# One core's attention and gated convolution with its hand-written order of operations exchanged for another, and part of its casts, copies and sums on other engines

## The chip, the cores and the metric

The kernel runs on one core of a Trainium2 chip. A core has four compute engines that work at the same time, each in the order of its own instruction list: TensorE (PE in the profile, with its weight loads shown as PEld), VectorE (DVE), ScalarE (ACT) and GpSimd (POOL). SyncE (SP) issues most of the DMA transfers. The engines wait for each other by semaphores. What is measured is the device time of one execution in microseconds (us); less is better.

## The reference

Attention over four batches of eight heads, 768 positions and 64 channels a head, and behind it a gated convolution. Heads marked in `is_retrieval` (0, 2 and 6) attend causally to all earlier keys; the others only to the first four keys and a window of the last 64.

```python
def _attn_ref(q, k, v, is_retrieval, n_sink, window):
    scores = scale * np.matmul(q, k.transpose(0, 1, 3, 2))
    ...
    scores = np.where(mask[None, :, :, :], scores, -1000000000.0)
    scores = scores - np.max(scores, axis=-1, keepdims=True)
    a = np.exp(scores)
    a = a / (np.sum(a, axis=-1, keepdims=True) + 1e-09)
    return np.matmul(a, v).astype(np.float32)

def _moe_ref(x, w_proj, filter_fft, w_out):
    proj = x @ w_proj
    x1, x2, x3 = (proj[..., :D].copy(), proj[..., D:2 * D].copy(), proj[..., 2 * D:].copy())
    X2 = np.fft.rfft(x2, n=S, axis=1)
    H = np.fft.rfft(filter_fft, n=S, axis=0)[None, :, :]
    x2_conv = np.fft.irfft(X2 * H, n=S, axis=1)
    y = x1 * x2_conv * x3
    return (y @ w_out).astype(np.float32)
```

All inputs and the output are float32; the flags are integers.

## The kernel before

**The fast path and its fallback.** `patterned` computes everything for the one pattern of retrieval heads that it was written for. At its end a flag `other` says whether the inputs had that pattern and whether the sums of the softmax were sane; all engines load it (L1314) and jump over the general path `general` if it is zero, as here, and meet at the closing barrier (L1394).

**The order is written out by hand.** Each operation of `patterned` is a small function with a name. The string `FAST` (L63 to L124) lists 994 names, and the loop over its words (L1307) calls them in that order, so the order of the words is the order of the instructions on every engine. A word may carry an engine letter behind a slash (`s`, or none, ACT; `v` DVE; `p` POOL) and a PSUM slot behind an @ sign (four slots of two banks each, shared by all tiles that TensorE writes). Operations that are tied to one engine have no letter. For the helper `scaled` (L687) a `p` is the same as no letter. No engine looks ahead in its list: an instruction that waits holds up all behind it on that engine. DMA issues stand in the list as well, on SP (loads and stores), POOL (weights and filter) or, for some last stores, ACT.

**Attention.** Heads are worked in 16 pairs `n` (four per batch; pair `n` belongs to batch `n // 4`), both heads of a pair beside each other on 64 rows. For a pair: loads `lq`, `lk`, `lv` on SP; casts `cq`, `ck` of q and k to bf16 (both in one, `cqk`, from pair 8 on), cast `cv` of v; copies `vx`, `vs` and `ks` set up the values and keys of the window and of the first four positions; `T` turns q and k so that channels lie on partitions. Pairs 0 to 7 are turned by TensorE (`T0.0`, `T0.1`, with the evictions `E0.0`, `E0.1` from PSUM), pairs 8 to 15 by a transposing DMA that SP issues (L962, one word `T12`). `sc12.1` are the score matmuls of one chunk (L990, 64 rows), `sb` adds the mask by matmul for the first four pairs, `ex` is the exponential on ACT (L1007), `mk` and `mr` the mask by product on DVE for the others (L1017 to L1037), `at` the product with the values (L1050), `rec` the reciprocal of the sums (L1056) and `nm` the division on DVE (L1067), which gives the tile f_attn.

**The transform.** The Fourier transform over the 768 positions is done by matmuls on sums and differences: `fd` and `fe` fold f_attn into halves, `fA`, `fS`, `fb` and `fr` fold these again for pairs 5 to 15, `W` (L1103 to L1111) multiplies with the tables and `We` evicts. In parallel `tn` turns f_attn back (by TensorE up to pair 10, by DMA after) and `te` evicts it into f_xT. Per batch `b`: `X` (L1154) projects in the transformed domain, `Xe` evicts, `pa`, `pb` and `pc` multiply with the filter's transform (tile f_HAB), `c` (L1227) transforms back, `ce` and `cv` (with two more indices) join the halves. `x1` and `x3` (L1189) are the other two projections, `xs` evicts x1, `g` and `y` form the gated product f_gy, `o` (L1262) multiplies by w_out, `oe` evicts and `st` stores.

**The filter.** `lfilt` (L776) loads 768 KB on POOL's queue. `fold0` and `fold1` (L793, L797, DVE) fold it, `F` (L805) transforms it, `H0.0` to `H2.2` (L691 on DVE, L693 on ACT) evict it scaled into f_HAB. `lw` loads w_proj in six parts, also from POOL.

**The end.** `rest` (L586) runs eight matmuls on zeros behind the last real ones. `gd0` to `gd4` (L655 to L674) work out the flag: three steps on DVE, a small matmul `gd3`, a last step `gd4`.

Of the kernel before, what the change touches and what calls it, by code (L numbers as in the profile page):

```python
# [78 lines left out]
sw0.1 lv6 E7.1/s sc6.0@1 nm5/v sc7.0@2 pa0.0/p H2.3 pa0.2/v rec4 ex6.0 x10.0.0@3 x10.0.1 ex7.0 x30.0.0@1 nm4/v H2.4
x30.0.1 xs0.0/s lq8 cv6/p sc7.1@2 lv7 ex7.1 ks7/s sc6.1@0 x10.2.1@3 pa0.1/v ex6.1 g0.0 ks6/p pb0.2/v x10.2.0 tn4@1  # L80
xs0.2/s vs6/s x30.2.0@2 lk8 fe5/p te4/v sc6.4@0 sc6.2@3 pc0.2/v pb0.0/v x10.1.1@1 fd5/v ex6.2 mk6.2 x10.1.0 Gk1 fS5/v
ex6.4 fA5/v x30.2.1 x10.3.1@3 sc7.2@0 xs0.1/s g0.2 sc6.3@1 cqk8/s x10.3.0 pc0.1/v ex6.3 fd4/v fr5 x30.1.1@2 fb5/v
xs0.3/s x30.1.0 c0.1.0@1 lk9 lq9 T8 ex7.2 mk6.0 fe4/p pc0.0/v W4.1@3 ce0.1/s mk6.1 mr6 cv7/s W4.0 g0.1 vx6/v We4/s
# [5 lines left out]
x11.0.1@2 fr6 x11.0.0 T9 oe0.3/s at8.0@1 at8.1 lq11 fS7/v fA7/v oe0.1/s fr7 xs1.0/s chk cv9/v vx9/v sc9.1@0 fb6/p
fb7/v rec8 T10 lv10 nm8/v fe8/p sc9.0@3 x11.3.1@2 x11.3.0 W7.1@1 ex9.1 W7.0 W6.0@0 fd8/p ks9/p ex9.0 xs1.3/v W6.1  # L90
sc10.4@3 sc10.3@2 cqk11/p We6/v mk9.1 vs9/s We7/s sc10.0@1 lv11 ex10.4 ex10.3 sc9.2@3 mk9.0 ex9.2 X1.1.1@0 mk9.2 T11
tn8@2 X1.1.0 fS8/v ex10.0 Xe1.1/s X1.2.0@3 at9.1@1 te8/s at9.0 sc10.1@0 ks10/p X1.2.1 fA8/v ex10.1 Xe1.2/s sc11.0@2
rec9 sc11.1@0 cv10/v cv11/p nm9/v st0.1 x31.0.1@1 mk10.1 lk12 ex11.0 fd9/p ex11.1 x31.0.0 X1.0.1@3 lq12 sw1.1 lv13
# [5 lines left out]
fS10/p fA10/p lk13 ex12.4 x12.0.1 ex12.0 x32.0.0@3 pb1.0/v lv12 fb10/p pc1.0/v xs2.0/s sc12.5@1 sc12.2@0 fd11/v  # L99
sc12.3@2 x32.0.1 ex12.5 c1.0.0@1 c1.0.1 ex12.2 fr10 fA11/v lq15 fS11/v W10.1@0 W10.0 ex12.3 fr11 c1.1.0@2 c1.1.1  # L100
fb11/p g2.0 ce1.0/s c1.2.0@3 We10/s ce1.1/s W11.0@0 cv1.0.1 cv13/p cv1.0.0 mk12.1 cv1.1.0 cv1.1.1 c1.3.1@1 cqk13/s
W11.1 c1.3.0 y1.1/v y1.0/v ce1.3/v lk14 We11/s c1.2.1 ce1.2/s cv1.3.0 X2.1.0@2 lk15 T13 cv1.3.1 cqk14/s cv1.2.1
cv12/s X2.0.0@0 X2.1.1 mk12.0 X2.0.1 x31.3.0@1 T14 mk12.2 Xe2.1/s x31.3.1 Xe2.0/s cv1.2.0 y1.3/v sc13.1@3 vs13/s
ex13.1 sc13.0@2 g1.3 cqk15/p at12.1@0 at12.0 pa2.0/p sc14.1@1 rec12 sc14.0@3 ex13.0 nm12/v vx13/s X2.2.0@2 y1.2/v
ks13/s X2.2.1 pb2.0/v o1.1.0@0 ex14.1 pa2.1/v T15 lv15 mk13.1 o1.1.1 ex14.0 sc13.2@1 sc15.0@3 mk13.0 pc2.0/v ks14/p
Xe2.2/s fe12/v ex13.2 sc15.1@2 mk13.2 o1.0.0 st0.5 ex15.0 o1.0.1 x12.3.0@1 pa2.2/v x12.3.1 pb2.1/v at13.1@3 ex15.1
at13.0 ks15/p tn12 oe1.1/s fd12/v rec13 xs2.3/s lv14 exp0 o1.4.0@2 o1.5.0 fS12/v sc14.4@0 nm13/v sw2.1 fA12/v
sc15.2@1 fe13/v sc14.3@3 fd13/v st0.3 ex14.4 sc14.2@0 ex15.2 o1.4.1 ex14.3 o1.5.1 x12.2.1@1 mk14.1 fS13/v fr12 ex14.2
fA13/v x12.2.0 cv14/v sw2.0 vs14/s cv15/v x12.1.0@3 o1.2.0@0 tn13 xs2.2/s mk15.0 vx15/s st1.1 mk14.0 o1.3.0 fb13/v
vs15/v fb12/v x12.1.1 oe1.5/s W12.1@1 mr14 mk15.1 fr13 mk14.2 W12.0 o1.3.1 o1.2.1 vx14/s at14.0@2 xs2.1/s mk15.2  # L110
W13.1@3 W13.0 st1.5 We12/s at14.1 oe1.3/s at15.0@1 pc2.1/v pb2.2/v We13/s at15.1 rec14 rec15 pc2.2/p x32.1.0@0
x32.1.1 nm14/v c2.1.0@3 nm15/v c2.1.1 tn14 st1.3 ce2.1/s g2.1 cv2.1.1 cv2.1.0 c2.0.0@2 ce2.0/s c2.2.1@1 fd14/p y2.1/v
c2.3.1@0 fe15/p c2.3.0 c2.2.0 ce2.3/s fd15/v x32.2.1@3 cv2.3.1 cv2.3.0 fe14/p c2.0.1 x32.2.0 cv2.0.1 tn15 fS15/p
fS14/p fA14/p x32.3.1@0 cv2.0.0 x13.1.1@2 fA15/p ce2.2/s x13.1.0 g2.2 x32.3.0 xs3.1/s fr14 fb15/v y2.0/v fb14/v
W14.0@3 W14.1 x13.0.1@2 We14/s cv2.2.0 fr15 x13.0.0 W15.0@3 W15.1 cv2.2.1 x33.0.1@1 We15/v x33.0.0 y2.2/p X3.2.1@3
X3.2.0 xs3.0/s Xe3.2/s X3.1.1@2 y2.3/v g3.0 X3.1.0 X3.0.1@1 sw3.1 g2.3 Xe3.1/s sw3.0 X3.0.0 x13.2.1@0 pa3.1/v Xe3.0/s
o2.1.0@3 x13.3.0@2 o2.0.0 pa3.2/p x33.2.0@1 x13.2.0 pb3.1/p x13.3.1 pb3.2/v gd0 pc3.2/v o2.1.1 xs3.2/s pa3.0/v
pb3.0/v x33.2.1 x33.1.0@0 pc3.1/v o2.0.1 xs3.3/s g3.2 c3.0.0@2 pc3.0/p x33.1.1 c3.1.0@1 oe2.1/s ce3.0/s o2.4.0@3 g3.1
# [1280 lines left out]
```

## Time and profile before

| | us |
| --- | --- |
| Median of 3 runs | 185.31 |
| Lowest and highest of them | 184.15 and 185.63 |
| Span of the profiled execution, first to last instruction | 182.1 |

The profile is of one execution; it gives the span of its instructions, and which of the runs it was, or what lay around the span in it, it doesn't say. The median lies 3.2 us above the span.

Busy time is given for each engine as a share of that span. Rows that name a line (L1189) give engine, operation, the tile written and the tiles read, the shape, how many there were, busy time in all and the mean of one in nanoseconds, and behind the second bar how long the engine had been idle before them and what ended it. `f_` stands before the names of the tiles. The chain of waits goes back from the last instruction to whatever released each step. In this profile the order of the list leaves no gaps on TensorE of more than a few tenths but these: the opening up to 14 us, some around 17 to 25 us, and one ahead of sc12.1 at 103 us.

### The profile page before, as it was taken

The numbers are of one execution on the slowest core, as the hardware profiler recorded it, in microseconds if no ns is written. First come the engines' busy times: TensorE is split into PE (matmuls) and PEld (weight loads), VectorE is DVE, ScalarE is ACT, GpSimd is POOL, SyncE is SP. The second block draws the span as 40 slices with busy tenths as digits, with TensorE's granted clock in tenths as the row PEclk, the third lists the DMA queues.
The fourth block names the chain that finished last, engine by engine and source line by source line (L and its number), as shares of the span: only waits on it lengthen the run. The fifth ranks groups of instructions, "written<-read, shape, count | busy, mean of one in ns | idle before, by whom it ended". The sixth has DMA issues, their size and how long they took to land.

```text
span 182.1 us, 4374 instructions
## 1 busy us (share of the span) xinstructions
PE 172.8 (95%) x1684; PEld 103.6 (57%) x1700; DVE 149.8 (82%) x298; ACT 145.3 (80%) x196; POOL 77.5 (43%) x94
## 2 busy tenths in 40 slices
...
GB/s 159 356 203 287 294 257 200 204 290 230 232 224 166 184 228 198 116 214 142 265 217 200 150 231 166 123 208 243 228 153 112 184 0 0 58 2 119 127 277 184
DMA packets 78396, 33.83 MB, mean 186 GB/s; under 512 B 67618, under 2 KB 74786, under 8 KB 78370
## 3 DMA queue, kind: packets, MB, share of 16 engines
...
q0 software_dynamic: 2944, 2.88, 9.8%
q8 instruction: 14, 0.23, 0.6%
q10 hardware_dynamic: 146, 0.13, 0.2%
...
## 4 chain that ended last, share of the span: by engine, by line
PE 82%; DVE 8%; ACT 4%; DMA 3%; issue 1%
PE f_x_ps L1189 23%; PE f_X_ps L1154 12%; PE f_out_ps L1262 10%; PE f_c_ps L1227 9%; PE f_sc L990 8%; PE f_att L1050 7%; DMA f_qkT<-f_qk_bf 3%; PE f_qkT_ps L952 2%; PE f_sc L1001 2%; PE warm L454 2%; PE f_xt_ps L1123 2%; ACT f_pT L1007 1%; DVE f_HAB L691 1%; PE f_W_ps L1103 1%; PE f_W_ps L1105 1%
## 5 line engine op out<-in xcount | busy, mean ns | idle before, releaser
L1007 ACT ACTIVATE f_pT<-f_sc 128x1024 bf16<-128x1024 f32 (+3 forms) x68 | 58.5, 914 | 3.6 <-PE f_sc L990 2.0
L1189 PE MATMUL f_x_ps<-f_xT,f_wproj 128*128 128x384 bf16 x256 | 46.9, 326 | 0.0
L1189 PEld LDWEIGHTS <-f_wproj 128*128 128x128 bf16 x256 | 23.9, 98 | 17.4 <-issue 1.6
L990 PE MATMUL f_sc<-f_qkT 64*128 64x128 bf16 (+3 forms) x328 | 20.9, 242 | 2.4 <-DMA f_qkT<-f_qk_bf 1.4
L1154 PE MATMUL f_X_ps<-f_wproj,f_xh 128*128 128x512 bf16 x90 | 22.1, 379 | 0.6 <-issue 0.2
L544 POOL TENSOR_TENSOR f_fo<-f_attn 128x384 bf16<-128x384 bf16 x15 | 14.6, 990 | 18.4 <-DVE f_attn L1067 17.3
L1262 PE MATMUL f_out_ps<-f_wout,f_gy 128*128 128x512 bf16 x86 | 22.0, 379 | 0.3
L990 PEld LDWEIGHTS <-f_qkT 64*128 64x128 bf16 x328 | 11.4, 94 | 13.0 <-issue 7.9
L1238 DVE TENSOR_TENSOR turns<-angle,f_c_ps 128x384 bf16<-128x384 f32 x32 | 16.3, 550 | 2.6 <-ACT angle L541 1.3
L1227 PE MATMUL f_c_ps<-f_Gi,f_P 128*128 128x384 bf16 x96 | 18.2, 326 | 0.1
L1050 PEld LDWEIGHTS <-f_pT 128*128 128x128 bf16 x472 | 16.2, 97 | 2.4 <-issue 0.4
L1050 PE MATMUL f_att<-f_v_aug,f_pT 128*128 128x65 bf16 x392 | 17.0, 193 | 0.0
L541 ACT COPY f_o<-f_out_ps 128x1024 f32<-128x1024 f32 (+2 forms) x15 | 12.1, 818 | 6.2 <-PE f_out_ps L1262 5.1
L541 ACT CAST f_X<-f_X_ps 128x1024 bf16<-128x1024 f32 x12 | 12.1, 1016 | 4.9 <-PE f_X_ps L1154 4.9
L1067 DVE TENSOR_TENSOR f_attn<-f_att,f_recs 128x768 bf16<-128x768 f32 x16 | 15.1, 951 | 0.6
L544 POOL TENSOR_TENSOR f_P<-f_X,f_HAB 128x1024 bf16<-128x1024 bf16 x4 | 8.9, 2215 | 14.5 <-ACT f_X L541 14.5
L544 POOL TENSOR_TENSOR f_gy<-turns,f_gy 128x768 bf16<-128x768 bf16 x5 | 8.5, 1710 | 14.6 <-DVE turns L1238 14.6
L1154 PEld LDWEIGHTS <-f_xh 128*128 128x128 bf16 x96 | 8.9, 97 | 10.2 <-issue 0.5
L1262 PEld LDWEIGHTS <-f_gy 128*128 128x128 bf16 x92 | 8.5, 98 | 8.8 <-POOL f_uv L544 0.4
L541 ACT COPY angle<-f_c_ps 128x384 f32<-128x384 f32 x15 | 7.2, 478 | 7.7 <-PE f_c_ps L1227 5.4
L1227 PEld LDWEIGHTS <-f_P 128*128 128x128 bf16 x96 | 9.1, 98 | 6.0 <-issue 0.2
L537 POOL CAST f_qk_bf<-qk_ahead 128x768 bf16<-128x768 f32 (+1 forms) x9 | 8.0, 900 | 8.7 <-DMA qk_ahead<-in_k_dram 3.4
...
## 6 DMA issues: line engine op xcount, KB each, us to landing
...
```

The costliest lines, as they stand in the source:

```text
L537: nc.gpsimd.tensor_copy(out=out, in_=in_)
L541: nc.scalar.copy(out=out, in_=in_)
L544: (nc.gpsimd if now["engine"] == "p" else nc.vector).tensor_tensor(out, a, b, op)
L990: nc.tensor.matmul(sc[:, bank, col:col + 128 * cnt], lhsT=keys, rhs=qkT(n)[rows, 0, 128 * i:128 * (i + cnt)], start=(col == 0 or not biase ...
L1007: nc.scalar.activation(out=pT(n)[:, c, :, 0:w], in_=held[f"sc.{n}.{c}"][:, :, 0:w], func=AF.Exp, scale=SCALE)
L1050: nc.tensor.matmul(att[:, hh, 65 * i:65 * i + 65], lhsT=pT(n)[:, c, bank, col:col + 128], rhs=values, start=(z == 0), stop=(z == len(here) ...
L1067: nc.vector.tensor_mul(attn(n).rearrange("p i hh d -> p hh i d"), rows[:, :, :, 0:64], recs()[:, n][:, :, :, None].to_broadcast([128, 2, N ...
L1154: nc.tensor.matmul(ps[:, u, :], lhsT=xh(b)[:, cc, chain, 128 * part:128 * part + 128], rhs=wproj()[:, cc, DM:2 * DM], start=(cc == 0), sto ...
L1189: nc.tensor.matmul(ps[:, s, 0:HS], lhsT=wproj()[:, cc, part * DM + cb * 128:part * DM + (cb + 1) * 128], rhs=xT(b)[:, cc, s * HS:s * HS + HS],
L1227: nc.tensor.matmul(ps[:, r, 0:HS], lhsT=P(b)[:, t, u, ch], rhs=Gi()[:, tile_no], start=(m == 0), stop=(m == 2))
L1238: fn(conv[:, half * HS:half * HS + HS], held[f"evs.{b}.{cb}"], held[f"c_ps.{b}.{cb}"][:, 1, 0:HS])
L1262: nc.tensor.matmul(ps[:, i % 2, :], lhsT=gy(b)[:, cb, i * 128:(i + 1) * 128], rhs=wout()[:, cb, :], start=(cb == 0), stop=(cb == NC - 1))
```

## The change

Only the string `FAST` is exchanged. The set of operations stays the same, word for word apart from letters and slots: 994 names. Their order is new from the first line to the last, and a part of them carries another letter: 100 words have `s` (119 before), 165 have `v` (153) and 74 have `p` (67). No function of the kernel is altered.

Among the words that have another engine: `ck0` (DVE to ACT), `fd0`, `fe0`, `vx1`, `vx2` and others of the small copies and sums (to POOL), `H0.0`, `H1.2`, `te3`, `Xe0.1`, `ce0.1`, `ce0.2` (ACT to DVE), `H2.2`, `We3` (DVE to ACT), `y3.2` (DVE to POOL). Among those that have another place: `lfilt` stands behind more of POOL's casts, `cqk12` and `T12` stand earlier among the matmuls of batch 1, and at the end `rest` stands ahead of `gd3` and `gd4`, with `gd1` and `gd2` near the end as well.

The lines of the string that hold these words:

```diff
 FAST = """
-mtab3 lq2 lk2 wrap0 size blank3@0 sin1 ck0/v lv0 T0.1@1 E0.1/s kz1/v sin2 cq0/p cos2 blank0@2 alt cos1 T0.0 lv1 gr1/s
-ck1/p blank2@3 ones0 E0.0/v cq1/p btab lq3 gs1/v gs0/p sc0.0@0 sc0.5@2 gc/p cq2/p sc0.2@3 sb0.5 sb0.0 ck2/p ex0.5
...
-sb1.0 cq3/p E2.0/s at0.0@3 at0.1 ks1/v lq5 gm1.2 sc2.1@2 Gk0 sc2.0@1 lfilt ex1.0 gm1.1 gm0.1 sb2.0 sb2.1 Gt0@0 rec0
...
-fd0/v E3.0/v lw1.0 ex2.4 lq6 sc2.3@3 at1.1@1 fe0/v sc2.2@0 at1.0 E3.1/v rec1 sb2.2 nm1/v ex2.3 W0.1@3 cv2/s cv3/p
...
-E4.0/s W1.1 tn2@1 lq7 vs3/v tn1@3 We1/s T4.1 te2/v sc5.0@1 sc5.1@0 lk6 te1/v at3.1@3 fold1 at3.0 E4.1/s fold0 rec3
...
-H0.2/s We2/s H2.2/v F1.1@3 F0.0 W3.1@0 H1.2/s lw0.0 H0.1/s H2.1/v ks5/p W3.0 cq6/v mk4.2 We3/v F1.0 H0.0/s H1.1/s
...
-X0.1.1 ex4.0 X0.0.1@0 ex4.1 mk4.1 ck6/v vx5/v tn3@3 lk7 mk4.0 vs5/v X0.0.0 Xe0.1/s te3/s mk5.2 T6.0@1 Xe0.0/s Hd1
...
-lk11 ex8.5 nm7/v y0.2/v x30.3.1@1 fe6/p ex8.1 x30.3.0 sc8.0@2 sc8.3@0 fd6/p g0.3 cqk9/s ex8.3 o0.1.0@3 o0.0.0 fd7/v
...
-x11.1.0@1 x11.1.1 o0.5.0 o0.4.1 o0.5.1 fb9/p vx11/s rec10 cqk12/s nm10/v at11.0@0 at11.1 fr9 te9/s fr8 fd10/p
-x31.1.0@3 T12 oe0.5/s W9.1@2 W9.0 xs1.1/s pb1.2/v x31.1.1 rec11 nm11/v tn10@1 pc1.1/v We9/s W8.1@0 tn11 W8.0 te10/s
-g1.1 pa1.0/v sc12.1@2 pa1.2/v sc12.4@3 x31.2.1@1 x31.2.0 We8/s sc12.0@0 fe10/v pc1.2/v fe11/p ex12.1 x12.0.0@2 g1.2
...
-gd1 c3.0.1 c3.2.1@0 c3.1.1 c3.2.0 o2.5.0 cv3.0.1 cv3.0.0 c3.3.0@2 ce3.1/s gd2 cv3.1.1 cv3.1.0 y3.0/p o2.5.1 o2.4.1
...
-cv3.3.0 x33.3.0 y3.2/v st2.5 st2.3 gd3@3 o3.0.0@2 o3.4.0@1 y3.3/v g3.3 gh o3.0.1 gd4 oe3.0/s o3.4.1 o3.1.0@0 o3.1.1
...
+wrap0 size ck0/s cos2 T0.1@2 mtab3 lk2 kz0/v cq0/v ones0 btab sin2 blank3@3 lq2 ck1/p cos1 T0.0 alt lv0 sin1 gr0/v
+cq1/p blank2@0 lk3 E0.1/v E0.0/s blank1@3 sc0.5@0 kz1/v gr1/s lv1 gm1.2 sc0.2@1 sb0.5 chk lq3 T1.1@3 gm0.1 ex0.5 sb0.2
...
+ex2.1 lq5 sc1.2@1 Gt1@2 ck3/p sb1.2 cq3/p ex2.0 T3.0@0 T3.1 ex1.2 Ge1/v sc2.4@2 ex2.4 fd0/p sc2.3@3 E3.0/v ex2.3
+sc2.2@1 sb2.2 ex2.2 lv3 E3.1/v vx1/p tn0@2 fe0/p at1.0@0 lk5 te0/v cq5/s at1.1 lq4 cv2/p ck4/p W0.1@2 cv3/s vx2/p
+sc3.1@3 sc3.0@1 lfilt vs2/p rec1 nm1/v sb3.0 at2.0@0 W0.0 ck5/p Gh1 fe1/v ex3.0 at2.1 ks3/s fd1/p sb3.1 We0/s lw1.1
...
+We1/s E4.0/s tn1@1 te1/v T4.1 fe2/p fold1 sc5.0@3 E4.1/s sc5.1@0 lv4 at3.1@1 lw1.0 ex5.0 ex5.1 fold0 at3.0 F2.1@2
...
+H0.0/v H1.0/v sc4.3@0 X0.2.0@3 lk7 ex4.3 H1.1/s ex5.2 mk4.2 lw0.0 X0.2.1 Xe0.2/s X0.1.0@0 H1.2/v mk5.2 Gk1 sc4.1@2
...
+T6.1@1 E6.1/s te3/v Xe0.1/v at5.0@3 sw0.0 lv7 ck7/p at5.1 mk4.0 lw2.0 lq8 T6.0 mk4.1 E6.0/s T7.1@2 rec5 pa0.0/p T7.0
...
+nm7/v x30.3.0@0 sc8.3@1 fe6/p y0.2/v sc8.0@3 cqk9/p x30.3.1 lk10 fd6/p tn7@2 y0.3/v ex8.3 ex8.0 cv8/v te7/s o0.0.0@1
...
+x11.1.1@3 mk11.2 Xe1.0/s mk10.2 o0.5.0@0 st0.1 fb8/p cqk12/s x11.2.1 mk10.0 o0.4.0 o0.4.1 o0.5.1 lk14 mr10 xs1.2/s
+tn9@1 fr8 x11.1.0 mk11.1 te9/s cv12/p vx11/v xs1.1/s at10.0@2 at10.1 T12 pb1.2/v pc1.2/v W9.0@1 W9.1 pa1.1/v at11.0@3
...
+sc12.1@2 fd10/v sc12.4@0 te10/s fd11/v x31.2.1@1 pb1.1/v We8/s x31.2.0 sc12.0@3 ex12.1 tn11 lv13 ex12.4 x12.0.0@2 g1.2
...
+cv3.2.1 o2.3.1 y3.2/p x33.3.1@1 oe2.3/s o3.4.0@2 x33.3.0 st2.3 o3.0.0@0 ce3.3/v cv3.3.1 cv3.3.0 y3.3/v g3.3 o3.4.1
...
+o3.5.0@3 oe3.3/s o3.5.1@2 oe3.6/v st3.2/v st3.3/v gd1 gd2 oe3.5/s late st3.6/s rest@1 gd3@1 gd4 st3.5/v exp0
```

More of the change, by code (lines that the diff above doesn't have):

```diff
@@ L79 @@
[L79 to L83, printed above, removed]
@@ L89 @@
[L89 to L93, printed above, removed]
@@ L99 @@
[L99 to L118, printed above, removed]
```

62 lines of the change are left out of this document (45 added, 17 removed).

## Prediction

> **What bounds the kernel now.** I read the page's busy shares and its chain first, then the same engines by stage (the view of windows, here five stretches of my choosing), then the chain piece by piece wherever it leaves the TensorE, then single rows for prices.
>
> ```profile
> PE 172.8 (95%) x1684; PEld 103.6 (57%) x1700; DVE 149.8 (82%) x298; ACT 145.3 (80%) x196; POOL 77.5 (43%) x94
> PE 82%; DVE 8%; ACT 4%; DMA 3%; issue 1%
> 14.30:33.60 19.30, 18.40 (x298) 13.22 (x300) 17.39 (x34) 18.61 (x27) 7.94 (x10) 1.00 1.13 252
> 33.60:73.20 39.60, 39.34 (x401) 23.27 (x401) 37.73 (x72) 37.40 (x51) 18.68 (x20) 1.00 1.10 216
> 73.20:104.00 30.80, 29.08 (x334) 18.65 (x334) 27.34 (x64) 28.80 (x35) 11.74 (x12) 1.00 0.98 188
> 104.00:140.00 36.00, 35.57 (x357) 21.48 (x358) 31.78 (x67) 33.29 (x44) 11.13 (x11) 1.00 0.92 187
> 140.00:177.50 37.50, 37.33 (x214) 20.75 (x216) 26.90 (x47) 16.05 (x24) 16.85 (x13) 1.00 0.33 95
> ```
>
> In the window rows the columns are the stretch, its length, then busy time (and count) of PE, PEld, DVE, ACT and POOL, the granted clock, the DMA share and GB/s. TensorE is the bound: 95% of the span, 82% of the chain, at clock 1.00 throughout. A new order of the same matmuls can win only what TensorE loses: 0.90 us in the first stretch (19.30 less 18.40), 0.26, 1.72, 0.43 and 0.17 in the next four, and some in the opening. What it can lose is larger, for three engines run nearly full beside TensorE: from 33.6 to 73.2 DVE is busy 37.73 of 39.60 and ACT 37.40. ACT and DVE have no slack there that a letter could use up unseen; POOL (18.68) has.
>
> The chain shows where TensorE waited:
>
> ```profile
> 19.37 0.62 DVE f_v_x L535
> ...
> 21.75 1.23 DVE f_fo L544
> ...
> 30.88 1.02 DVE f_xT L535 x2
> 31.90 0.86 DVE f_fold L797
> ...
> 39.50 0.97 DVE f_xh L535
> ...
> 98.13 5.49 DMA f_qkT<-f_qk_bf
> 103.62 0.05 issue
> 103.66 0.61 PE f_sc L990 x6
> ```
>
> From 19.4 on and again from 30.9 to 40.5 the chain goes over DVE; at 98.13 it goes over one transposing DMA, T12, which score sc12.1 then waits for.
>
> **The change, part by part.** It alters only the string `FAST`: the same 994 words, in another order, some with another engine letter or PSUM slot. By the code ACT goes from 192 to 172 instructions, DVE from 284 to 296, POOL from 79 to 87 (those the string issues). TensorE's matmuls are the same. The prices that the moved words need:
>
> ```profile
> L541 ACT COPY angle<-f_c_ps 128x384 f32<-128x384 f32 x15 | 7.2, 478 | 7.7 <-PE f_c_ps L1227 5.4 <-DVE turns L1238 2.2
> L535 DVE COPY angle<-f_c_ps 128x384 f32<-128x384 f32 x1 | 0.5, 545 | 0.0
> L535 DVE CAST f_qk_bf<-qk_ahead 128x768 bf16<-128x768 f32 x4 | 2.3, 574 | 0.0
> L537 POOL CAST f_qk_bf<-qk_ahead 128x768 bf16<-128x768 f32 x8 | 6.5, 822 | 5.6 <-DMA qk_ahead<-in_k_dram 3.4 <-DMA qk_ahead<-in_q_dram 2.1
> L544 DVE TENSOR_TENSOR f_fo<-f_attn 128x384 bf16<-128x384 bf16 x17 | 6.8, 407 | 0.1
> L544 POOL TENSOR_TENSOR f_fo<-f_attn 128x384 bf16<-128x384 bf16 x15 | 14.6, 990 | 18.4 <-DVE f_attn L1067 17.3 <-DVE f_br L1095 1.1
> L535 DVE COPY f_xT<-f_xt_ps 128x768 bf16<-128x768 bf16 x4 | 2.1, 552 | 0.4 <-PE f_xt_ps L1123 0.3
> L691 DVE TENSOR_SCALAR f_HAB<-f_F_ps 128x1024 bf16<-128x1024 f32 x1 | 1.2, 1218 | 0.0
> L535 DVE COPY f_qkT<-f_qkT 128x16 bf16<-128x16 bf16 x2 | 1.0, 521 | 0.0
> L880 POOL MEMSET f_v_x<- 64x520 bf16 x1 | 0.5, 524 | 0.0
> L544 DVE TENSOR_TENSOR f_gy<-turns,f_gy 128x768 bf16<-128x768 bf16 x7 | 5.1, 734 | 0.1
> L544 POOL TENSOR_TENSOR f_gy<-turns,f_gy 128x768 bf16<-128x768 bf16 x5 | 8.5, 1710 | 14.6 <-DVE turns L1238 14.6
> L1017 DVE TENSOR_TENSOR f_pT<-f_pT,mtab 128x512 bf16<-128x512 bf16 x9 | 3.6, 420 | 1.1 <-ACT f_pT L1007 1.1
> ```
>
> 1. *Fewer borders between score blocks and other matmuls.* The old TensorE order has 38 runs of scores, the new one 35, so six borders go. A border costs a row like the 0.05 us of issue ahead of sc12.1: **-0.3** (0 to -0.6, were each twice as dear).
>
> 2. *From the opening to the fold.* The sums fd0 and fe0 (the 1.23 us that DVE puts in the chain at 21.75) and the copies vx1, vx2 go to POOL, cast ck0 goes to ACT. TensorE lost 0.90 us here, so at most that comes back, and only if it survives the fold. The fold needs the filter:
>
> ```profile
> L776 POOL DMA_DIRECT2D f_filt<-in_moe_filter_fft_dram x1: 1037/1037/1037, 18.9 to 18.9; - x1
> DMA to landing us min/median/max: 12.7/12.7/12.7
> q0 software_dynamic: 2944, 2.88, 9.8%
> ```
>
> Issued at 18.9, it landed at about 31.6, and DVE folded at 31.9, its queue full up to there. In the new order POOL first does fd0 and fe0 (0.99 each), vx1 and vx2 (copies with no row on POOL: between nothing and the 0.82 of a cast; I take the 64x520 memset's 0.52), cv2 and ck4 (casts, 0.82 each): 2.0 + 1.0 + 1.6 = 4.6 us, less up to 0.7 by which an earlier opening starts them. So the issue comes some 4 us later, near 22.9. Behind it on POOL stand vs2, ck5 and lw1.1; behind fold1 on DVE, which works in order, stand rec3, nm3 and all that follows. When it lands is the largest unknown. At the row's 12.7 us it lands at 35.6: +3.7. The transfer itself is short: GpSimd's queue moved 2.88 MB in 9.8% of the span (17.8 us of all 16 engines), so 768 KB are 4.8 us of them; the rest of the 12.7 was sharing with other loads, two of which (lq6, lv5) the new order puts behind the fold. Had it the engines alone, it would land near 28. The middle of 28 and 35.6 is 31.8, no lateness; but the DMA share stays above 1.0 here, so I lean to the upper half: **+0.4** (-0.9 to +3.7).
>
> The Trainium skill bears on this ("DMA: Bandwidth & Descriptors", section "Anatomy of one DMA — SWDGE (gpsimd) path"): it fits one transfer from GpSimd as 2.0 us plus its bytes at 436 GB/s. That is 3.8 us for this one (an estimate from that page), against the 12.7 measured here in company; by the page the filter would be there before 27 and the term would be -0.9.
>
> 3. *DVE from rec3 to nm7* (33.6 to 73.2 now). Words that leave DVE there: the negated H2.2 (1.22 by the f_HAB row), casts cq6, ck6, ck7, cv5 (0.57 each: 2.3), We3 (the f_xh piece of the chain, 0.97) and y0.3 (0.73): 5.2 us. Words that come: H0.0 (1.22), H1.2 (half as wide: 0.6), Xe0.1 (1024 wide; no DVE row, so the f_HAB row's 1.22; its ACT time isn't far), te3 (0.55), fe3 and fe4 (0.41 each), ks5, ks6, ks7 (0.52 each), ce0.1 and ce0.2 (0.545 each): 7.1 us. Of small ones, fA5 and vx6 go and vs6, vx7 and Gk0 come: one more, at most 0.5, say 0.3. Net +2.2 on an engine that has 1.87 us of idle, of which 1.1 is a wait for ACT (the mask row) that a lighter ACT can end sooner. So **+1.0** (0 if all idle is used and the rest hidden; +2.2 if none). TensorE feels it at tn7, which needs nm7: between at7.1 and tn7 the old list has two x30.3 products, two scores and five pieces of o, the new one only the first four, so less covers a late nm7.
>
> 4. *T12.* Its cast cqk12 stays on ACT but stands earlier before sc12.1.
>
> ```profile
> PE f_sc L990 <- DMA f_qkT<-f_qk_bf: 1.4, 1, 1.4
> 96.48 1.30 PE f_x_ps L1189 x8
> ```
>
> Between cqk12 and sc12.1 the new list has four x products where the old has two, and three pieces of o and two of attention besides. At 1.30 us for eight matmuls, two products are 1.3 us, and with the rest the 1.4 of the wait (1.72 idle in that stretch) is covered: **-1.5** (-0.9 if DMA traffic makes the 5.49 longer). What is late next there is DVE, which gets fb9 and fd9 from POOL and is at 27.34 of 30.80.
>
> 5. *104 to 140.* TensorE lost 0.43; ACT gets lighter and DVE heavier (ce1.0, ce1.2, vx13): **-0.2** (-0.4 to +0.6).
>
> 6. *The end.*
>
> ```profile
> 177.65 1.73 PE f_rest_ps L586 x8
> L1314 POOLq TENSOR_LOAD <-other x1: 764/764/764, 173.5 to 173.5; - x1
> L1394 POOLq DRAIN  x3: 40/107/803, 175.7 to 181.8; - x3
> L1394 POOLq EVENT_SEMAPHORE  x4: 17/17/17, 181.3 to 182.0; - x4
> ```
>
> y3.2 goes from DVE (0.73) to POOL (1.71), and o3.4.0, which multiplies by it, follows after one x product (0.65) and one matmul of 512 columns (0.22, an eighth of `rest`): 0.84 uncovered, where the old list has more between: **+0.6** (0 to +1.0). Then the readiness chain: `rest` (eight filler matmuls) now stands ahead of gd3 and gd4, which before ran long in front of it. All engines load the flag `other` and branch on it. POOL did so at 173.5 and had drained 3.0 us later (175.7 + 0.8), hidden. In the new order gd4 ends about 1.73 + 0.6 us after `rest` starts (0.6 is my estimate for gd3, gd4 and their handovers); POOL's 3.0 end 5.3 after it and the closing barrier of 0.8 (181.3 to 182.1) follows: 6.1, where the span now ends 4.45 after `rest` starts (182.1 less 177.65). Some of POOL's way to its drain may run ahead of the load, so of the 1.65 I take **+1.3** (0 if the landing of the stores sets the end in any case, +1.65).
>
> Sum: -0.3 + 0.4 + 1.0 - 1.5 - 0.2 + 0.6 + 1.3 = **+1.3** on the profiled span of 182.1, so 183.4. The page gives the span only; the runs (184.15 to 185.63) lie 2.1 to 3.5 above it, the median 3.2. On the median's scale: 185.3 + 1.3 = **186.6**.
>
> **The rivals.** (a) *The filter is late*: it lands by the 12.7 us row, and fold, rec3 and DVE's full stretch move with it. It decides once it lands after about 32.9 (0.6 later than my sum has it, there 1% is passed). For it: the row, the DMA share over 1.0. Against it: the loads moved behind. In place of +0.4 stand up to +3.7, less what DVE's 1.87 of idle takes up: 188.0 to 189.9, centre 189.0.
>
> (b) *Faster*: TensorE keeps its 0.9 from the first stretch (the filter is no later than DVE), DVE's additions find its idle time (0), T12 is covered, and the flag's chain ends inside the wait for the last stores (+0.2 left): -0.3 - 0.9 - 1.5 - 0.2 + 0.6 + 0.2 = -2.1, 183.2. For it: every stretch where TensorE idles is touched by the new order. Against it: the flag now waits for the last matmul.
>
> (c) *POOL blocks DVE*:
>
> ```profile
> 83.76 2.43 DVE L1025 TENSOR_TENSOR f_pT<-f_pT,mtab 128x768 bf16<-128x768 bf16 x3
> L1025 DVE TENSOR_TENSOR f_pT<-f_pT,mtab 128x768 bf16<-128x768 bf16 x6 | 3.9, 658 | 0.0
> 83.11 1.47 POOL L537 CAST f_qk_bf<-f_qk_f 128x1536 bf16<-128x1536 f32 x1
> ```
>
> Three masks took 2.43 us while POOL's cast ran, where the other three took 3.9 - 2.4 = 1.5: 0.9 lost to one cast. With eight more POOL instructions beside a fuller DVE, two such losses inside part 3 add about 1.8: 188.4.
>
> The Trainium skill says why ("GPSIMD Engine Reference", "Key points"): GpSimd shares its SBUF interfaces with VectorE, and collides with DVE instructions that have two SBUF inputs. The trace agrees; by that rule the masks and sums suffer, the PSUM evictions don't.
>
> (d) *Nothing gained or lost*: the losses of part 6 are hidden and the gain of T12 is eaten by part 3: 185.3 or near it.
>
> **How the numbers follow.** About 1% is what a measurement can tell from no change: below 183.46 faster, above 187.16 slower. Forecast 0.30, (d) 0.12, (a) 0.23, (c) 0.13, (b) 0.22. So faster 0.22, same 0.42, slower 0.36. The range leaves about a tenth on each side: 183.2 (the whole of b) to 189.2 (just past the centre of a). The likeliest case alone spans 185.5 to 187.1.
>
> **What would show it.** In the profile after: a T12 row with no wait of sc12.1; f_filt's landing, and fold1's start against 31.9; DVE busy without idle between rec3 and nm7, and TensorE waiting at tn7 or te7; POOL's drain on the flag after 181 and the span ending 6 us after `rest`. I am wrong if the fold starts by 31.5 and the span still grows, if TensorE idles where none of these is, or if the stretch of part 3 is no longer than now.

## The result, and the profile after

The changed kernel takes 204.96 us (median of 4 runs, 202.37 to 205.55) against 185.09 us before (4 runs, 184.15 to 185.63). The ratio is 1.1105 (95% interval 1.0983 to 1.1227): slower by 11%, some 20 us. The forecast was 186.6 us with a range up to 189.2. The profiled execution, the longest of the four at 205.55 us, has a span of 204.1 us, 22.0 more than before. Some runs of a kernel are a percent or two longer than the others, this one among them, and a ratio is formed from the others alone, so it can differ a little from that of the medians. Line numbers of the kernel after are one lower than before's (L1017 is L1016).

The head of the page after: span, busy shares, TensorE's granted clock in 40 slices, and the chain's shares by engine.

```profile
span 204.1 us, 4375 instructions
...
PE 177.0 (87%) x1685; PEld 104.8 (51%) x1700; DVE 168.1 (82%) x310; ACT 135.6 (66%) x176; POOL 84.0 (41%) x102
...
PEclk9976999999999999999999999999999999999996
...
PE 41%; DVE 37%; ACT 10%; issue 5%; DMA 2%; POOL 1%; DVEq 0%; ACTq 0%
```

TensorE no longer sets the end alone. Its share of the chain is halved (82% before), and VectorE has 37% of it (8% before). VectorE is busy 18.3 us longer for 12 more instructions. And the clock dips in the third and fourth slice and in the last, which no slice did before.

To place the loss I divided the traces at four points that every order has: where `rec3` starts, where `nm7` ends, where `sc12.1` starts and where `rest` starts. In each stretch up to `rest` the four traces have the same number of matmuls to within two. The table has the length of each stretch and, in brackets, how long TensorE was idle in it (all in us; e7 and e14 are experiments below).

| | start to `rec3` | to `nm7` | to `sc12.1` | to `rest` | to the end |
| --- | --- | --- | --- | --- | --- |
| before | 33.5 (4.0) | 39.6 (0.3) | 30.5 (1.7) | 73.8 (0.6) | 4.6 (2.7) |
| after | 38.1 (7.9) | 47.8 (6.8) | 29.7 (0.3) | 79.1 (4.7) | 9.3 (7.2) |
| e7 | 34.3 (6.0) | 47.6 (6.9) | 31.2 (1.6) | 79.9 (5.3) | 4.8 (2.9) |
| e14 | 33.9 (5.9) | 44.0 (3.4) | 30.1 (0.6) | 76.7 (2.6) | 4.9 (3.0) |

After has four places of loss: 4.6 us up to `rec3`, 8.2 from there to `nm7`, 5.3 between `sc12.1` and `rest`, and 4.7 behind `rest`. Ahead of `sc12.1` it gains 0.8.

**The opening.** The chain of waits after, from 9.97 us on (start, length, what):

```profile
9.97 0.73 DVE zeros L645
...
10.91 0.78 DVE differs L648
11.69 0.02 issue
11.72 0.15 DVE differ L649
11.87 0.46 DVE f_G L727
12.32 0.88 DVE f_qkT L534
13.20 0.04 issue
13.24 0.80 PE f_qkT_ps L951 x6
```

These are the steps of `chk`, the comparison of the flags with the pattern. Before, it stood in the middle of the kernel; the new order has it in the first three lines, ahead of an eviction from PSUM that TensorE waits for. The prediction does not mention it. The windows after, in the prediction's columns:

```profile
11.00:13.00 2.00, 0.00 (x0) 0.00 (x0) 1.97 (x4) 1.47 (x2) 1.85 (x5) 0.82 0.96 269
13.00:15.00 2.00, 1.76 (x11) 0.97 (x11) 1.11 (x3) 0.06 (x1) 1.65 (x4) 0.50 0.99 241
17.00:19.00 2.00, 2.00 (x18) 1.66 (x17) 0.00 (x0) 1.53 (x2) 0.83 (x1) 0.50 0.90 266
...
38.10:85.90 47.80, 40.99 (x401) 23.43 (x402) 43.97 (x76) 34.72 (x46) 20.27 (x20) 1.00 1.08 192
```

TensorE does nothing for two microseconds and then works at half the clock. The last row is the stretch from rec3 to nm7, part 3 of the prediction: 47.8 us where it was 39.6, for the same 401 matmuls. TensorE is idle for 6.8 us of them (47.80 less 40.99) where it was 0.26, and VectorE is busy for 43.97 us where it was 37.73.

**What VectorE does there.** Two places of the timeline after (start, length, engine, line, operation, tiles):

```profile
53.79 2.12 POOL L543 TENSOR_TENSOR f_P<-f_X,f_HAB 128x1024 bf16<-128x1024 bf16 x1 [2.92 <-ACT f_X L540]
...
53.85 2.68 DVE L1016 TENSOR_TENSOR f_pT<-f_pT,mtab 128x512 bf16<-128x512 bf16 x2
...
132.67 2.13 POOL L543 TENSOR_TENSOR f_m<-f_X,f_HAB 128x1024 bf16<-128x1024 bf16 x1 [5.74 <-ACT f_X L540]
...
132.73 2.48 DVE L543 TENSOR_TENSOR turns<-turns,f_x1s 128x768 bf16<-128x768 bf16 x1
```

The two masks and the product begin just behind a product on GpSimd (53.79 + 2.12 = 55.91; 132.67 + 2.13 = 134.80) and end only after it (56.53 and 135.21). The product's rest, 135.21 less 134.80, is 0.41 us, not far below what one takes by itself (0.567 on average before), and the two masks' is 0.62 (two of 0.42 before). So VectorE's instruction hardly moves until GpSimd's is through. The groups of VectorE's instructions by form, after:

```profile
L1016 DVE TENSOR_TENSOR f_pT<-f_pT,mtab 128x512 bf16<-128x512 bf16 x9 | 5.4, 630 | 0.0
...
L543 DVE TENSOR_TENSOR turns<-turns,f_x1s 128x768 bf16<-128x768 bf16 x3 | 4.3, 1444 | 0.0
...
L755 DVE TENSOR_SCALAR f_Gh<-f_G 128x6 bf16<-128x6 bf16 x1 | 1.7, 1685 | 0.0
```

The means were 420, 567 and 221 ns before. I counted VectorE's records that last over 250 ns longer than the shortest with the same operation, tiles and shapes in the traces of before and after: 10 before, 7.3 us too long in all; 24 after, 18.0 us. Each of the 24 began while an instruction of GpSimd ran. It matters where they lie: of before's 10 only two stand on the chain of waits, with 1.3 us of the 7.3; of after's 24 it is 17, with 14.1 us of the 18.0.

**The filter.** Three answers on single tiles after: its issue, its landing, and the fold.

```profile
L775 POOL DMA_DIRECT2D f_filt<-in_moe_filter_fft_dram x1: 1039/1039/1039, 27.7 to 27.7; - x1
...
DMA to landing us min/median/max: 7.5/7.5/7.5
...
L796 DVE TENSOR_TENSOR f_fold<-f_filt x1: 949/949/949, 36.2 to 36.2; 128x1536 bf16<-128x1536 bf16 x1
```

Issued 8.8 us later than before, the filter had landed at 35.2 (27.7 + 7.5) and waited for the fold, not the fold for it.

**The end.** The chain's last pieces after:

```profile
194.93 1.74 PE f_rest_ps L585 x8
...
196.91 0.20 DVE other L673
```

The flag is ready at 197.1, behind `rest`. The instructions that read it (L1313) and those of the closing barrier (L1393), after, with durations in ns and the first and last start:

```profile
L1313 ACTq TENSOR_LOAD <-other x1: 476/476/476, 197.2 to 197.2; - x1
L1313 POOLq TENSOR_LOAD <-other x1: 506/506/506, 197.2 to 197.2; - x1
...
L1393 POOLq DRAIN  x3: 40/107/807, 202.4 to 203.8; - x3
L1393 ACTq DRAIN  x2: 8/44/79, 198.3 to 203.5; - x2
```

All engines load the flag at 197.1 to 197.2, ScalarE drains 1.1 us later, GpSimd 5.2 us later, and its drain and the barrier end the span at 204.1.

### The profile page after: what moved, and what is told of

Read it like the earlier page. It is cut to its first block, busy times and chain, and to the rows that moved or that the text cites. A ratio compares the mean times of both kernels' runs of the same rounds, so it can differ in the third digit from the quotient of the medians.

```text
span 204.1 us, 4375 instructions
## 1 busy us (share of the span) xinstructions
PE 177.0 (87%) x1685; PEld 104.8 (51%) x1700; DVE 168.1 (82%) x310; ACT 135.6 (66%) x176; POOL 84.0 (41%) x102
## 3 DMA queue, kind: packets, MB, share of 16 engines
q0 software_dynamic: 2944, 2.88, 10.8%
## 4 chain that ended last, share of the span: by engine, by line
PE 41%; DVE 37%; ACT 10%; issue 5%; DMA 2%; POOL 1%; DVEq 0%; ACTq 0%
PE f_x_ps L1188 10%; PE f_out_ps L1261 6%; PE f_c_ps L1226 5%; DVE f_P L543 4%; PE f_X_ps L1153 4%; DVE f_qkT L534 4%; PE f_sc L989 4%; PE f_att L1049 3%; DVE f_attn L1066 3%; ACT f_pT L1006 3%; DVE turns L1237 2%; DVE f_pT L1024 2%; PE f_sc L1000 2%; DVE f_m L543 2%; ACT f_xh L540 2%
## 5 line engine op out<-in xcount | busy, mean ns | idle before, releaser
L1188 PE MATMUL f_x_ps<-f_xT,f_wproj 128*128 128x384 bf16 x256 | 48.0, 326 | 1.9 <-DVE f_xT L534 1.9
L989 PE MATMUL f_sc<-f_qkT 64*128 64x128 bf16 (+2 forms) x328 | 22.0, 247 | 4.9 <-DVE f_gy L1211 1.3
L1261 PE MATMUL f_out_ps<-f_wout,f_gy 128*128 128x512 bf16 x87 | 23.4, 380 | 0.4
L989 PEld LDWEIGHTS <-f_qkT 64*128 64x128 bf16 x328 | 11.8, 95 | 16.5 <-issue 12.6
L543 POOL TENSOR_TENSOR f_fo<-f_attn 128x384 bf16<-128x384 bf16 x13 | 12.3, 947 | 16.4 <-DVE f_attn L1066 16.4
L540 ACT COPY f_o<-f_out_ps 128x1024 f32<-128x1024 f32 (+2 forms) x13 | 10.7, 834 | 9.6 <-PE f_out_ps L1261 6.7
L543 POOL TENSOR_TENSOR f_gy<-turns,f_gy 128x768 bf16<-128x768 bf16 x4 | 6.5, 1637 | 21.2 <-DVE turns L1237 11.4
L540 ACT CAST f_xh<-f_W_ps 128x768 bf16<-128x768 f32 x14 | 11.2, 809 | 5.5 <-PE f_W_ps L1106 4.0
L540 ACT CAST f_X<-f_X_ps 128x1024 bf16<-128x1024 f32 x11 | 11.1, 1013 | 5.5 <-PE f_X_ps L1153 5.5
L536 POOL CAST f_qk_bf<-qk_ahead 128x768 bf16<-128x768 f32 (+1 forms) x10 | 9.8, 982 | 9.3 <-DMA qk_ahead<-in_q_dram 3.8
L951 PE MATMUL f_qkT_ps<-identity,f_qk_bf 128*128 128x128 bf16 x96 | 8.1, 236 | 5.4 <-DVE f_qkT L534 2.5
```

The source lines that it names most:

```text
L536: nc.gpsimd.tensor_copy(out=out, in_=in_)
L540: nc.scalar.copy(out=out, in_=in_)
L543: (nc.gpsimd if now["engine"] == "p" else nc.vector).tensor_tensor(out, a, b, op)
L989: nc.tensor.matmul(sc[:, bank, col:col + 128 * cnt], lhsT=keys, rhs=qkT(n)[rows, 0, 128 * i:128 * (i + cnt)], start=(col == 0 or not biase ...
L1188: nc.tensor.matmul(ps[:, s, 0:HS], lhsT=wproj()[:, cc, part * DM + cb * 128:part * DM + (cb + 1) * 128], rhs=xT(b)[:, cc, s * HS:s * HS + HS],
L1261: nc.tensor.matmul(ps[:, i % 2, :], lhsT=gy(b)[:, cb, i * 128:(i + 1) * 128], rhs=wout()[:, cb, :], start=(cb == 0), stop=(cb == NC - 1))
```

## The experiments

Each kernel is timed against the kernel before on the same chip; its median and its ratio are given. Unless it says otherwise, words that are not shown stay as in the base that is named. Where a diff has words of the string alone, one word stands on a line.

**Order and letters apart.** e1 is the new order with before's letters, e2 the old order with the new letters (108 words differ). The diff is e1's, against after; e2's against before is its reverse.

```diff
-ck0/s
-fd0/p
-H0.0/v
+ck0/v
+fd0/v
+H0.0/s
...
```

> The new order of the words with all engine letters of the kernel before. Theory A (letters: more work on GpSimd, which holds up VectorE's reads from SBUF, 12 us more lengthening on VectorE than before): most of the 20 us go, 186 to 192 us. Theory B (order: the flags' check in the opening, the flag behind the last matmul, too little lead between producers and consumers): 197 to 205 us, with the clock drop between 11 and 20 us and the 9 us behind the last matmuls still there.

> The order of the kernel before with the new engine letters. Theory A (letters): 195 to 203 us, VectorE's busy time near the 168 us of the changed kernel. Theory B (order): 184 to 188 us, although VectorE is busier. Both at once, each making the other worse: between, and the two single effects add up to less than 20 us.

e1: 225.88 us, ratio 1.2297 (1.2234 to 1.2360). e2: 204.74 us, ratio 1.1206 (1.1117 to 1.1295). Either half alone costs as much as the whole or more: 42 and 21 us, where both together cost 20. The two do not add up; the new order needs its letters, and the old order does not stand the new letters.

**The letters in two groups**, both in the old order: e5 takes the 69 words that come to GpSimd or leave it, e6 the 39 that move between ScalarE and VectorE (`ck0/v` to `ck0/s`, `H0.0/s` to `H0.0/v`, `te3/s` to `te3/v` and so on). Of e5, against before:

```diff
-vx1
-fd0/v
-y3.2/v
+vx1/p
+fd0/p
+y3.2/p
...
```

> The order of the kernel before; only the 69 words that go to GpSimd or come from it take their new letter. If GpSimd's part (its slow operations, and VectorE held up beside it) is what the letters cost: most of the 21 us of all letters together, 198 to 204 us. If it is the swaps between ScalarE and VectorE: 184 to 190 us.

> The order of the kernel before; only the 39 words that swap between ScalarE and VectorE take their new letter. If GpSimd's part is the cost: 184 to 190 us. If every letter set against its order costs alike: 39 of 108 letters, some 8 us, 190 to 194 us.

e5: 193.21 us, ratio 1.0486 (1.0410 to 1.0562). e6: 196.80 us, ratio 1.0670 (1.0592 to 1.0748). In the old order the groups add up: 0.0486 + 0.0670 = 0.116, and e2 has 0.121. So GpSimd's letters are somewhat under half of the letters' price; plain moves between ScalarE and VectorE are the rest (26 words to VectorE, 13 to ScalarE).

**`chk`.** e3 is after with `chk` back in the middle; e18 is before with `chk` brought into the opening, ahead of `kz0`. The diff is e3's, against after.

```diff
 sb0.5
-chk
 lq3
...
 xs1.0/s
+chk
 fr7
```

> The changed kernel with only the check of the flags (eight small VectorE instructions) put back from the opening to where it stood before. If it is what let TensorE idle 2.5 us at 11 us and brought the clock to 0.5 for some 7 us: 200 to 202 us (3 to 5 less), no idle of over 1 us on TensorE in the opening and clock 1.00. If POOL's late casts hold the opening up anyway: 204 to 205 us and the clock drop stays.

> The kernel before with only the check of the flags moved into the opening, ahead of kz0 and E1.0 on VectorE. If eight small instructions there cost by themselves what the changed kernel lost (TensorE idle 2.5 us, clock at 0.5 for some 7 us): 187 to 190 us, with a stretch of clock under 1 between 11 and 20 us. If they hide: 184 to 185 us, clock 1.00.

e3: 203.25 us, ratio 1.1000 (1.0930 to 1.1070), 0.0105 or 1.9 us under after's, less than the two intervals resolve. e18: 184.78 us, ratio 1.0000 (0.9945 to 1.0055). Its windows, to be set beside after's, where TensorE was idle and its clock fell to 0.50; here it is busy 1.71 and 2.00 us, at 1.00:

```profile
11.00:13.00 2.00, 1.71 (x15) 0.86 (x16) 1.43 (x3) 2.00 (x3) 2.00 (x4) 1.00 0.69 136
13.00:15.00 2.00, 2.00 (x30) 1.43 (x29) 1.33 (x3) 1.63 (x3) 2.00 (x5) 1.00 0.92 206
```

In the old order `chk` hides beside a busy TensorE; in the new one it stands ahead of what TensorE waits for. The step by itself is harmless, its place is not.

**The flag.** e4 is after with `gd1` to `gd4` ahead of the last outputs.

```diff
 st1.5
+gd1
...
 st2.1
+gd2
...
+gd3@3
 o3.1.0@3
 o3.1.1
+gd4
...
 st3.3/v
-gd1
-gd2
 oe3.5/s
 late
 st3.6/s
 rest@1
-gd3@1
-gd4
 st3.5/v
```

> The changed kernel with only the chain of the flag (gd1 to gd4) put ahead of the last outputs again. If the flag sets the end: 4 to 5 us less, 200 to 201 us, and the span ends 4 to 5 us after the filler matmuls start instead of 9. If the landing of the last stores sets it: within 1 us of the changed kernel.

199.76 us, ratio 1.0861 (1.0798 to 1.0923): 0.0244 under after's ratio, 4.5 us. The readers of the flag and GpSimd's drains in e4:

```profile
L1313 POOLq TENSOR_LOAD <-other x1: 500/500/500, 192.4 to 192.4; - x1
...
L1393 POOLq DRAIN  x3: 40/107/807, 196.9 to 200.6; - x3
```

GpSimd again takes 4.5 us from load to drain, but now while TensorE still works, and 5.0 us lie between `rest` and the end instead of 9.3.

**Three things undone**: e7 has e3's and e4's edits, and the filter's issue ahead of `fd0`.

```diff
 ex2.4
+lfilt
 fd0/p
...
 sc3.0@1
-lfilt
 vs2/p
```

> The changed kernel with the flags' check late, the flag's chain early, and the filter's load issued ahead of fd0. If the three are separate costs: 204.9 less 4.5 to 5 (flag) less 1.5 to 3 (check) less 0 to 1 (filter, which did not end VectorE's waits): 196 to 199 us, so 12 to 15 us remain. If the filter is what delays the fold: 193 to 195 us.

199.32 us, ratio 1.0840 (1.0753 to 1.0926). Against e4 this is 0.0021, 0.4 us, nothing that can be told apart: neither the filter nor `chk` is worth much once the flag is early. The traces show why for `chk`: e3 reaches `rec3` 3.0 us ahead of after (35.1 and 38.1) but `rest` only 1.5 ahead (193.3 and 194.8). e7 is the base of what follows: 15 us are left that are neither flag, `chk` nor filter.

**What leaves GpSimd.** e8 gives eleven of GpSimd's largest words in e7 to VectorE; e9 gives nine of VectorE's back to ScalarE (`H0.0`, `H1.2`, `te3`, `Xe0.1`, `ks7`, `vs6`, `vx7`, `ce0.1`, `ce0.2`), e10 all 26 that the change took from ScalarE to VectorE, e11 the 11 that it took from ScalarE to GpSimd, and e12 both of these. Of e8, against e7 (the others change the letters of the words named in the same way, to `s`):

```diff
-pa0.0/p
-pb2.0/p
-y3.2/p
+pa0.0/v
+pb2.0/v
+y3.2/v
...
```

> As the kernel with three undone, and the eleven large products and sums on GpSimd (pa, pb, pc, y) on VectorE, which does each in 0.55 to 0.7 us. If VectorE loses more to GpSimd's large operations than it would take to do them: 3 to 6 us less than with three undone, and VectorE's busy time does not rise. If they were free on GpSimd: VectorE gets 7 us more work and the time grows by 2 to 5 us.

> The kernel with three undone (199.3 us), and nine words between the fold and nm7 that went from ScalarE to VectorE (H0.0, H1.2, te3, Xe0.1, ks7, vs6, vx7, ce0.1, ce0.2) back on ScalarE. Theory DVE-bound: VectorE is busy 9.6 to 9.8 of 10 us from 50 to 70 us, so taking 5.7 us off it gives 3 to 6 us: 193 to 196 us. Theory order: each engine's list is a chain through the others, and a letter against the order costs about what it relieves: 198 to 203 us.

> The same with all 26 words that went from ScalarE to VectorE back on ScalarE (some 15 us less on VectorE). Theory DVE-bound: 188 to 194 us. Theory order: 200 to 212 us, since the new order with all old letters took 225.9.

> The kernel with three undone, and the eleven copies and casts that went from ScalarE to GpSimd back on ScalarE. If GpSimd's copies lengthen VectorE's work and that is on the path: VectorE's busy time falls by 3 to 6 us and the time by 2 to 5 us, 194 to 197 us. If not: 198 to 203 us.

> All 37 words back on ScalarE, which then has about the work it had before. If VectorE's load and its lengthening are the whole of what is left: 185 to 190 us. If the order itself is what costs: over 197 us, with VectorE no longer full and TensorE waiting all the same.

| run | us | ratio | interval |
| --- | --- | --- | --- |
| e8 | 199.61 | 1.0785 | 1.0685 to 1.0885 |
| e9 | 202.20 | 1.1031 | 1.0849 to 1.1213 |
| e10 | 204.54 | 1.1141 | 1.0924 to 1.1357 |
| e11 | 201.33 | none | none |
| e12 | 208.69 | 1.1383 | 1.1224 to 1.1542 |

For e11 no ratio is formed; its four runs lie between 199.20 and 203.82. None of them helps by more than its interval; e12 costs more than e7, e10 by its median too. A lighter VectorE with a heavier ScalarE is worse in this order, as e1 says of all letters at once. e8 shows something besides, in the busy row of its page:

```profile
PE 177.0 (89%) x1685; PEld 104.5 (53%) x1700; DVE 167.0 (84%) x321; ACT 135.7 (68%) x176; POOL 62.8 (32%) x91
```

VectorE does eleven more products, six of some 0.7 us and five of 0.55 (their means in e14's profile), and is busy only 0.8 us longer than in e7 (166.2): it saves nearly as much in drawn-out instructions as it takes on. So moving work off GpSimd does not show what the collisions cost. For that the work has to vanish.

**GpSimd's instructions cut short.** In e13 (after), e14 (e7), e17 (e2) and e15 (before) most of GpSimd's casts, copies, sums and products work on the first eighth of their elements only, which leaves seven eighths of that work out: 47 of the 74 words, and 46 of the 67 in e15. All instructions and their order stay; some of the tiles are kept for all pairs instead of made anew.

```diff
+    def eighth(ap):
+        if now["name"] not in SHORT:
+            return ap
...
     def two(out, a, b, op):
+        if now["engine"] == "p":
+            out, a, b = eighth(out), eighth(a), eighth(b)
```

> The changed kernel with the same instructions on every engine in the same order, but 47 of GpSimd's 74 instructions in the list work on an eighth of their elements only (the rest of the data is left as it was; those tiles are kept instead of made anew). If GpSimd holding up VectorE is what costs: VectorE's lengthening falls from 24 us to under 12 and the time by 9 to 13 us, 192 to 196 us. If the order's tight handovers cost by themselves: 202 to 206 us, since GpSimd was idle 59% of the time and is nowhere the one waited for.

> The same on the kernel with three undone (199.3 us). Lengthening theory: 187 to 191 us, within 2 to 4% of before. Order theory: 197 to 201 us.

> The same on the kernel before (46 of 67). Its VectorE instructions are lengthened too (7.3 us in ten instructions), but hardly where the chain runs. Lengthening theory: 0 to 2 us less than before, no more. If shorter GpSimd work helps any kernel by itself: 5 us or more.

> The order of the kernel before with the new letters (204.7 us), and GpSimd's work cut to an eighth in 47 of 74 words as in the other such runs. If lengthening is what the letters cost: 185 to 190 us. If about half of it is (as in the changed kernel, which gained 7 to 8 us of 20): 194 to 199 us, the rest being letters that stand where the order gives their engine no time.

| run | base | us | ratio | interval | base's ratio |
| --- | --- | --- | --- | --- | --- |
| e13 | after | 197.70 | 1.0750 | 1.0682 to 1.0817 | 1.1105 |
| e14 | e7 | 191.46 | 1.0440 | 1.0363 to 1.0516 | 1.0840 |
| e17 | e2 | 196.32 | 1.0616 | 1.0500 to 1.0732 | 1.1206 |
| e15 | before | 184.69 | 1.0005 | 0.9959 to 1.0052 | 1 |

The busy row of e14's page:

```profile
PE 174.0 (92%) x1685; PEld 103.2 (54%) x1700; DVE 153.6 (81%) x310; ACT 135.6 (72%) x176; POOL 47.8 (25%) x102
```

The groups, of the masks and of the product that took 630 and 1444 ns in after:

```profile
L1029 DVE TENSOR_TENSOR f_pT<-f_pT,mtab 128x512 bf16<-128x512 bf16 x9 | 3.5, 414 | 0.0
...
L556 DVE TENSOR_TENSOR turns<-turns,f_x1s 128x768 bf16<-128x768 bf16 x3 | 2.0, 658 | 0.0
```

The same 310 instructions keep VectorE busy 12.6 us less than in e7 (166.2), the masks are back at 414 ns, and of the drawn-out instructions 4 are left, 2.3 us. The time falls by 0.040 of before's, 7.4 us. In the kernel before, the same cut takes 6.2 us of busy time off VectorE (149.8 to 143.6) and gains nothing; eight of its ten drawn-out instructions lie where the chain does not run.

The cut also ends GpSimd's own work earlier. In e7 this is hardly what counts. These are the shares of its chain of waits by engine:

```profile
DVE 40%; PE 36%; ACT 10%; issue 7%; DMA 4%; SPq 2%; DVEq 0%
```

No instruction of GpSimd stands on that chain, but 14 drawn-out ones of VectorE do, 12.1 us too long in all. In the old order with the new letters (e2) it may well count, for 9.7 us of that chain are GpSimd's own work beside 10.7 us on drawn-out instructions. There the cut takes away 0.059 (e17 against e2), and the 0.062 that are left are near the 0.067 of e6, which has the swaps between ScalarE and VectorE alone.

**T12.** e16 is before with cqk12 and T12 set further up, behind `ex11.2` and ahead of the eviction `xs1.2` on ScalarE.

```diff
 ex11.2
+cqk12/s
+T12
 tn9@3
...
 rec10
-cqk12/s
 nm10/v
...
 x31.1.0@3
-T12
 oe0.5/s
```

> The kernel before with only the words cqk12 and T12 moved ahead of xs1.2, so that the transposing DMA is issued some 3 us sooner. If the 1.4 to 1.5 us wait of sc12.1 is worth its length: 1.0 to 1.5 us less than before. If the cast's 1.5 us on ScalarE then holds up xs1.2 and what follows: within 0.5 us of before.

184.83 us, ratio 1.0055 (1.0016 to 1.0094). No score waits for the transposing DMA any more, but the chain of e16 now has, some nine microseconds earlier:

```profile
89.21 5.72 DMA qk_ahead<-in_q_dram
...
95.22 1.19 issue
96.40 0.80 ACT angle L540
...
97.25 1.46 PE f_x_ps L1188 x8
```

The cast that was moved up waits 0.2 us on ScalarE for its own load and takes 1.47 us, and the eviction behind it (L540, 96.40) comes that much later: TensorE stands 1.1 us ahead of the product at 97.25. Moved in this way, the wait has only changed its place.

## Why the prediction was wrong

The forecast of 186.6 us was wrong in sign and size. Its steps one by one:

- **Step 1, fewer borders (-0.3)**: not seen apart; nothing of that size decides here.
- **Step 2, the filter (+0.4), and rival (a)**: wrong about the cause. The issue came at 27.7 instead of the estimated 22.9, but the load took 7.5 us instead of 12.7, and the fold, late for other reasons, did not wait. e7 issues it earlier and gains nothing that can be measured. The estimate of 3.8 us from the Trainium skill ("DMA: Bandwidth & Descriptors", section "Anatomy of one DMA — SWDGE (gpsimd) path") is below both measured figures.
- **What stands in no step**: `chk` in the opening. The prediction names other words of the opening and not this one, and so misses TensorE's gap at 11 us and the halved clock behind it. Its price lies between 0.4 us (e7 against e4) and 1.9 (e3 against after), inside the intervals.
- **Step 3, VectorE from rec3 to nm7 (+1.0, at most +2.2)**: the step that failed most. The place was right, but the stretch grew by 8.2 us, with TensorE idle for 6.8 us of it instead of 0.26. The price was summed from durations by engine, as if an instruction cost the same wherever it stands, and as if only the sum on the fullest engine counted. Both are refuted. VectorE was to be busy for 2.2 us more there and was for 6.2 (43.97 less 37.73). In e14, with GpSimd's work short, it is 1.5 more:

```profile
33.85:77.85 44.00, 40.57 (x401) 23.28 (x402) 39.20 (x76) 34.67 (x46) 10.93 (x20) 1.00 1.05 208
```

So the sum of the moved words was near enough, and what it left out are the instructions drawn out behind GpSimd's. Cutting these short takes 3.6 us off the stretch (47.6 in e7 to 44.0). The other 4.4 us are still there with no engine busy for more than 40.6 of the 44.0, so the sum on the fullest engine does not give them either. e6, which moves no work to or from GpSimd, costs 6.7% in the old order, and giving VectorE's words back to ScalarE (e12, with the copies) makes e7 slower.
- **Step 4, T12 (-1.5)**: right at its place. From nm7 to sc12.1 TensorE is idle for 0.3 us instead of 1.7, 1.4 less, and the stretch is 0.8 us shorter. What was gained is lost behind it, in step 5. e16 shows that in the old order the cast costs on ScalarE what the earlier DMA saves.
- **Step 5 (-0.2)**: wrong sign. From sc12.1 to the end of nm15 the stretch grew from 36.7 to 40.0 us, with TensorE idle for 3.9 us instead of 0.4 and VectorE busy for 38.0 instead of 32.5. In e14 it is 37.2 us.
- **Step 6, the end**: mechanism right, size wrong. `other` was ready 2.2 us after `rest` began (197.1 less 194.93; 2.3 forecast). GpSimd then took 5.2 us to its drain and 0.8 for it, where I had taken 3.0 in all from before's row and even discounted that. Instead of +1.3 this term is +4.5 (e4), 4.7 in the trace. The +0.6 for y3.2 was about right. It is the one product of GpSimd there, it stands on the chain, and TensorE's weight load waits 0.4 us for it:

```profile
187.23 1.65 POOL f_gy L543
188.88 0.05 issue
188.93 0.39 PE f_out_ps L1261
```

- **Rival (c), GpSimd holds up VectorE (1.8 us, chance 0.13)**: the right mechanism, much too cheap. I took two losses from one row; after has 24 drawn-out instructions, and cutting GpSimd's short gives back 6.5 us in after (1.1105 less 1.0750) and 7.4 in e7. The signs stood in the prediction's own lines. The 1.23 us of f_fo at 21.75 in the chain, which step 2 took for the price of fd0 and fe0, are one sum drawn out behind a cast on GpSimd, where 17 such sums take 407 ns on average. Two of the rows for prices are means with such an instruction in them: 521 ns (one of 876, one of 166) for the copies ks5 to ks7, and 734 ns (six of some 553, one of 1819) for the y. The rows also correct a sentence of it: not only masks and sums suffer. The one-input f_Gh of 128x6 took 1685 ns, and a comparison of eight numbers in `chk` (`differs`) 0.77 us, where the kernel before has 153 ns for the same step. The Trainium skill has the wider rule: "GPSIMD Engine Reference", section "Key points", lists VectorE's instructions in a 2-port mode beside those with two inputs, and "Trainium Architecture — The Big Picture", section "What this means for kernel authors", calls the sharing an exclusive lock and no split of bandwidth. The product at 132.73, which lasts until GpSimd's has ended and then 0.41 us more, agrees with the lock.

The account of the 20 us, in before's 185: the late flag 4.5 (shown by e4), `chk` 0.4 to 1.9, VectorE's instructions drawn out behind GpSimd's about 7 (shown by e13, e14 and the chain of e7, and e15 as the counter-test). In e14, which has none of these losses but a rest of the collisions, 7 to 8 us remain (191.46 against 184.33; 0.044 by the ratio). By the table 4.4 of them lie between rec3 and nm7 and 2.9 between sc12.1 and `rest`. e1, e2, e5, e6 and e9 to e12 bear on them: the new order with the old letters costs 42 us, the old order with the new letters 21, and giving letters back in part gains nothing. Which handovers these 8 us consist of is not settled. No version tried is faster than the kernel before.
